# First batch's elementwise steps on VectorE, U and V converted in the first pair, later loads issued behind the turning transfers

## The chip, the cores and the metric

The kernel runs on one core of a Trainium2 chip. The metric is the device time of one execution in microseconds (us). The engines named below are TensorE (PE, with its weight loads as PEld), VectorE (DVE), ScalarE (ACT), GpSimd (POOL) and SyncE (SP, which here only issues transfers).

## What is computed

Three stages follow one another on four batches of 768 positions and 384 features. The first is a recurrence over time with a complex decay for each head and feature (its state is 48 x 48 for each of 8 heads), the second a mixing step of rank 32 (U and V) with a two-layer network, the third a two-dimensional Fourier transform, a normalisation and a second two-layer network:

```python
for t in range(S):                       # attention, q, k, v, a_re, a_im: (4, 8, 768, 48)
    S_re, S_im = ar*S_re - ai*S_im + kv, ar*S_im + ai*S_re     # a scaled to at most 0.999
    y[:, :, t] = einsum('bhd,bhde->bhe', q[:, :, t], S_re)
x = y.transpose(0, 2, 1, 3).reshape(B, S, H * D)
u = x + (x.transpose(0, 2, 1) @ U @ V).transpose(0, 2, 1)      # moe
x = u + relu(u @ w_ch1) @ w_ch2                                # w_ch1: 384 x 1536
u = x + real(fft(fft(x, axis=1), axis=2))                      # moe2
un = (u - mean(u)) / sqrt(var(u) + 1e-6)
out = u + relu(un @ w_ch1) @ w_ch2
```

## The kernel before

**Tiling.** Time is cut into 6 chunks of 128 positions for each batch, taken two at a time as a pair `m` (m = 0, 1, 2 are batch 0, m = 3, 4, 5 batch 1, and so on). For a pair, `decays(m)` makes the running products of the decay's size (a square, Ln, Exp, a scan along time, Ln, Exp) on tiles of 128 x 768 and multiplies q and k by them; `turns(m)` makes the running angle (Arctan, a scan, a reduction to one turn, Sin and Cos), and multiplies q and k by sine and cosine into one tile `QK` for each chunk. Six transfers for each chunk (`moved`, on SP's queue, the turning transfers) lay `QK` out again as `QT`. `products(m, j)` works on a chunk with TensorE: `scores` (tile `sc`), the mask (`pm`, VectorE), `kp` (a transpose of k, copied by ScalarE to a tile `k`), the output `y` from `pm` and from the state `S`, and the state's next value through `g`. The state runs from chunk to chunk: `S` of chunk c needs `S` of chunk c-1, and `y` of chunk c+1 needs `S` of chunk c and `QT` of chunk c+1.

**Order of the work.** Batch 0's attention is a preamble (`first_attention`): only when all its six chunks are done does the first network pass start. From then on the network's matmuls of batch b (`moe_units`: `hp`, `hh`, `hl`, `acc`) have the attention of batch b+1 woven between them. The instructions of each engine are put in order before the run by a scheduler that simulates the program with priorities; `tc.issue_after(i)` keeps one instruction behind another one, and `kept`, `tabled` and `behind` are helpers that use it. Each engine takes its instructions strictly in that order, so one that waits holds up all behind it. SP's queue too is one order for all loads, turning transfers and stores.

**Buffers that set the pace.** The weights `w` and also U and V come as pairs of 32-bit words, three tiles `st` in turn hold them (`stw0_f_z`: network 0, slice f of 12, half z), and `from_f64` turns them to floats: one step on ScalarE (`wx`), three on VectorE, then `load_w` splits them with ScalarE and GpSimd. The tiles `k` of the attention use the same three buffers. `QT` of chunk 5 lies in the buffer of chunk 2, that of chunk 4 in the buffer of chunk 1, so their transfers wait until `y` of chunk 2 and of chunk 1 is done. In batches after the first, the inputs `ain` and `qkin` have one buffer each.

**What the change touches.** `decays` has, for m = 2, a way of its own with squares on GpSimd, and `parts` of batch 0 that run on GpSimd (L402, L423, L424). `load_uv` is called inside `chunks()`, after the first pair. Loads (`fetch`, `load`, `load_v`) are plain `nc.sync.dma_start`, placed on SP by the scheduler. 20 and 36 `warm` matmuls stand at set places in TensorE's order.

Of the kernel before, what the change touches and what calls it, by code (L numbers as in the profile page):

```python
# [23 lines left out]
NC = 6  # L24
# [22 lines left out]
def mixer_kernel(ctx, tc, a_in, qk_in, v_in, u_in, v4_in, w_in, cc_in, ss_in, cb_in, sb_in, id_in, mask_in, rows_in, out):  # L47
# [75 lines left out]

    def fetch(src, name):
# [145 lines left out]
    def load(kind, m):  # L270
# [9 lines left out]
        nc.sync.dma_start(t, {"a": a_in, "qk": qk_in}[kind][b, cs[0] // 2])  # L280
# [26 lines left out]
    def parts(m):  # L307

        return [slice(0, 1), slice(1, 2)] if m == 0 else [slice(0, 2)]

    def decays(m):
# [26 lines left out]
        at_once = b or m in (0,1,)  # L338

        def sooner(m, *args, **kw):  # L340

            if m == 3:
                with tc.issue_after(last[0]):
# [11 lines left out]
        def least_re(js):  # L355

            (re,) = of(js, a[:, 0])
            V.tensor_scalar(unread(js), re, RE_LEAST, 0.0, ALU.is_ge, ALU.add, accum_out=stat("re", b, cc[js.start]))

        def most_im(js):  # L360
            (s2_,) = of(js, s2)
            V.tensor_scalar(unread(js), s2_, IM_MOST**2, 0.0, ALU.subtract, ALU.max, accum_out=stat("im", b, cc[js.start]))

        for js in jj:
            re, im, s1_, s2_ = of(js, a[:, 0], a[:, 1], s1, s2)
            if at_once:
                if b == 0:
                    V.scalar_tensor_tensor(out=s2_, in0=im, scalar=0.25, in1=im, op0=ALU.mult, op1=ALU.mult)
                else:
                    sooner(m, s2_, im, AF.Square, scale=0.5)  # L370
                sooner(m, s1_, re, AF.Square, accum_out=stat("big", b, cc[js.start]))
                if m == 0:
                    steady(js)
                else:
                    unused = unread(js) if b == 0 else Th[:, :, js]
                    sooner(m, unused, re, AF.Relu, bias=least, scale=-1.0, accum_out=stat("im", b, cc[0]))
                    sooner(m, unused, s2_, AF.Relu, bias=most, accum_out=stat("im", b, cc[1]))
                V.scalar_tensor_tensor(out=s1_, in0=s2_, scalar=4.0, in1=s1_, op0=ALU.mult, op1=ALU.add)
            else:
                (V if m == 0 else G).tensor_tensor(s2_, im, im, ALU.mult)  # L380
# [903 lines left out]
```

## Time and profile before

| | us |
|---|---|
| median of 3 runs (lowest, highest) | 955.83 (954.43, 956.68) |
| the profiled execution | 958.05 |
| its span, first to last instruction | 956.2 |
| PE busy | 827.8 (87%) |
| DVE, ACT, POOL busy | 605.2, 409.0, 238.1 |

The profile's 40 slices of 23.9 us show TensorE at 0 to 2 tenths busy in the first three slices, at 7 to 8 up to about 220 us and at 8 or 9 from there. The first network matmul (`hp`) stands at 150.08 us. The chain of work that ended last is by line mostly network matmuls (six lines of 6% each); the preamble has its place in the rest of it. A row of a timeline gives the start, the duration, the engine, the line, the operation, output and inputs with shapes, and in brackets the idle time of the engine before it with what ended it.

### The profile page before, as it was taken

The numbers are of one execution on the slowest core, as the hardware profiler recorded it, in microseconds if no ns is written. First come the engines' busy times: TensorE is split into PE (matmuls) and PEld (weight loads), VectorE is DVE, ScalarE is ACT, GpSimd is POOL, SyncE is SP. The second block draws the span as 40 slices with busy tenths as digits, with TensorE's granted clock in tenths as the row PEclk, the third lists the DMA queues.
The fourth block names the chain that finished last, engine by engine and source line by source line (L and its number), as shares of the span: only waits on it lengthen the run. The fifth ranks groups of instructions, "written<-read, shape, count | busy, mean of one in ns | idle before, by whom it ended". The sixth has DMA issues, their size and how long they took to land.

```text
span 956.2 us, 16800 instructions
## 1 busy us (share of the span) xinstructions
PE 827.8 (87%) x6686; PEld 564.4 (59%) x6686; DVE 605.2 (63%) x1118; ACT 409.0 (43%) x769; POOL 238.1 (25%) x289
## 2 busy tenths in 40 slices
PE   0227678778898899999999999899999999999997
PEld 0216565546575676566775566567666765766664
DVE  5795869786568677667347757853556666574121
ACT  5556347765567875674232443322112212211111
POOL 2060335542012121201027334711321322110000
PEclk9997689988899998999999999999999999999999
DMA  9508454836727765573336331300210111000000
GB/s 367 69 5 114 130 142 144 172 74 107 142 66 119 141 110 136 83 106 85 68 119 221 109 100 60 99 25 1 67 55 13 50 35 50 1 26 26 2 25 28
DMA packets 47095, 83.43 MB, mean 87 GB/s; under 512 B 5600, under 2 KB 36064, under 8 KB 47008
## 3 DMA queue, kind: packets, MB, share of 16 engines
q1 hardware_dynamic: 45152, 75.96, 34.5%
q0 software_dynamic: 1856, 6.31, 1.8%
q8 instruction: 54, 0.88, 0.4%
q14 instruction: 33, 0.27, 0.1%
HBM read 53.79 MB, written 9.44 MB: 66 GB/s over the span
## 4 chain that ended last, share of the span: by engine, by line
PE 48%; DVE 18%; ACT 8%; DMA 7%; issue 4%; POOL 3%; SPq 2%; DVEq 0%; POOLq 0%; ACTq 0%
PE acc L212 6%; PE acc L213 6%; PE hp L103 6%; PE hp L104 6%; PE hp L105 6%; PE acc L198 6%; DMA stw<-in_w_dram 3%; PE sc L530 3%; DMA QT<-QK 2%; ACT ls L99 2%; SPq L445 2%; DVE ls L404 2%; PE y L555 2%; DVE hl L231 1%; ACT turn L99 1%
## 5 line engine op out<-in xcount | busy, mean ns | idle before, releaser
L231 DVE SCALAR_TENSOR_TENSOR hl<-hp,hh 128x384 f16<-128x384 f32 x192 | 105.2, 551 | 177.3 <-ACT hh L230 176.7
L230 ACT ACTIVATE hh<-hp 128x384 f16<-128x384 f32 x192 | 93.0, 487 | 273.9 <-PE hp L105 250.9
L212 PE MATMUL acc<-w,hh 128*128 128x384 f16 x576 | 191.0, 332 | 5.3 <-ACT hh L230 5.3
L213 PE MATMUL acc<-w,hh 128*128 128x384 f16 x576 | 190.5, 331 | 1.7 <-POOL w L166 1.7
L198 PE MATMUL acc<-w,hl 128*128 128x384 f16 x576 | 128.0, 330 | 0.0
L103 PE MATMUL hp<-u,w 128*128 128x384 f16 x288 | 94.7, 330 | 10.9 <-DVE hl L231 8.0
L103 PE MATMUL hp<-n,w 128*128 128x384 f16 x288 | 94.0, 326 | 2.3 <-DVE hl L231 2.3
L530 PE MATMUL sc<-QT 96*128 96x128 f32 x384 | 66.2, 329 | 34.1 <-DMA QT<-QK 19.2
L104 PE MATMUL hp<-u,w 128*128 128x384 f16 x288 | 95.4, 331 | 0.0
L105 PE MATMUL hp<-u,w 128*128 128x384 f16 x288 | 95.2, 331 | 0.0
L105 PE MATMUL hp<-n,w 128*128 128x384 f16 x288 | 94.0, 326 | 0.0
L104 PE MATMUL hp<-n,w 128*128 128x384 f16 x288 | 93.9, 326 | 0.0
L104 PEld LDWEIGHTS <-w 128*128 128x128 f16 x576 | 56.7, 98 | 48.3 <-issue 13.7
L212 PEld LDWEIGHTS <-hh 128*128 128x128 f16 x576 | 56.8, 99 | 46.1 <-ACT hh L230 9.2
L530 PEld LDWEIGHTS sc<-QT 96*128 96x128 f32 x384 | 59.1, 234 | 40.1 <-issue 27.2
L198 PEld LDWEIGHTS <-hl 128*128 128x128 f16 x576 | 56.8, 99 | 39.0 <-issue 1.9
L103 PEld LDWEIGHTS <-w 128*128 128x128 f16 x576 | 56.5, 98 | 39.4 <-issue 3.1
L105 PEld LDWEIGHTS <-w 128*128 128x128 f16 x576 | 56.6, 98 | 37.5 <-issue 1.0
L213 PEld LDWEIGHTS <-hh 128*128 128x128 f16 x576 | 57.0, 99 | 32.7 <-issue 2.1
L540 PE MATMUL kp<-ident,QK 128*128 128x128 f32 x120 | 23.2, 317 | 51.3 <-DVE QK L497 35.9
L164 ACT ACTIVATE w<-wxw 128x384 f16<-128x384 f32 x48 | 24.8, 522 | 63.9 <-DVE wxw L143 63.8
L165 POOL TENSOR_SCALAR wxw<-wxw 128x384 f32<-128x384 f32 x48 | 33.1, 690 | 73.1 <-ACT w L164 72.5
(276 smaller groups left out, 1569.3 us busy)
## 6 DMA issues: line engine op xcount, KB each, us to landing
QT<-QK SPq DMA_DIRECT2D x144, 129.0 KB
stw<-in_w_dram SPq DMA_DIRECT2D x48, 384.0 KB
ain<-in_a_dram SPq DMA_DIRECT2D x12, 768.0 KB
qkin<-in_qk_dram SPq DMA_DIRECT2D x12, 768.0 KB
x1d<-x SPq DMA_DIRECT2D x24, 192.0 KB
vin<-in_v_dram SPq DMA_DIRECT2D x18, 192.0 KB
lo<-x1d SPq DMA_DIRECT2D x12, 192.0 KB
out_dram<-lo SPq DMA_DIRECT2D x12, 192.0 KB
```

Source lines behind the costliest of these rows:

```text
L99: ordered(lambda: A.activation(*args, **kw))
L103: T.matmul(o, ah, bh, start=start, stop=False, skip_group_check=skip)
L104: T.matmul(o, ah, bl, start=False, stop=False, skip_group_check=skip)
L105: T.matmul(o, al, bh, start=False, stop=stop, skip_group_check=skip)
L164: A.activation(w[:, 0, zs], x, AF.Copy, scale=WP[z])
L165: G.tensor_scalar(x, x, WP[z], 0.0, ALU.mult, ALU.add)
L198: T.matmul(acc[t], hl[:, t * 128 : (t + 1) * 128], w2h, start=False, stop=f == FB - 1 and extra is None)
L212: T.matmul(acc[t], hh[:, ts], w2h, start=f == 0, stop=False)
L213: T.matmul(acc[t], hh[:, ts], w2l, start=False, stop=False)
L230: A.activation(hh, hp, AF.Relu)
L231: V.scalar_tensor_tensor(out=hl, in0=hp, scalar=0.0, in1=whole_of(hh), op0=ALU.max, op1=ALU.subtract)
L530: T.matmul(ps[:, h, :], q[:, 128:256], q[:, :128], start=True, stop=True)
```

## The change

1. Batch 0's elementwise steps leave GpSimd: the squares and the sum of m = 2 take the same way as those of m = 1, and L402, L423 and L424 of batch 0 run on VectorE. Batches 1 to 3 keep GpSimd there.
2. In the first pair the check `steady` goes behind the sum on VectorE; the square at L412 of batch 0 is put into ScalarE's fixed order, ahead of the angles' table load; the checks with Relu of m = 1, 2 come behind it.
3. U and V are loaded right behind the first pair's inputs, ahead of those of pairs 1 and 2, and converted while the first pair is worked on.
4. Every load written down after the first turning transfer (`later`) is issued behind the last turning transfer that the program has written down by then.
5. `turns(2)` is woven one step behind `turns(1)`, and `decays(3)` starts 8 steps later in the program.

```diff
+    def later(to, x):
+        if lastqt[0] in nc.cur_bb.bb.instructions:
+            with tc.issue_after(lastqt[0]):
+                nc.sync.dma_start(to, x)
+        else:
+            nc.sync.dma_start(to, x)
...
-        nc.sync.dma_start(st.rearrange("p n w -> p (n w)"), src.bitcast(I32))
+        later(st.rearrange("p n w -> p (n w)"), src.bitcast(I32))
...
-        nc.sync.dma_start(t, {"a": a_in, "qk": qk_in}[kind][b, cs[0] // 2])
+        later(t, {"a": a_in, "qk": qk_in}[kind][b, cs[0] // 2])
...
-            nc.sync.dma_start(t, v_in[b, c])
+            later(t, v_in[b, c])
...
-            if m == 3:
-                with tc.issue_after(last[0]):
+            if m == 3 or m in (1, 2) and args[2] == AF.Relu:
+                with tc.issue_after(last[0] if m == 3 else squared[0]):
...
+            V.scalar_tensor_tensor(out=s1_, in0=s2_, scalar=4.0, in1=s1_, op0=ALU.mult, op1=ALU.add)
+            if m == 0:
+                with tc.issue_after([i for i in nc.cur_bb.bb.instructions if i.engine == V.engine][-1]):
                     steady(js)
...
-            else:
-                (V if m == 0 else G).tensor_tensor(s2_, im, im, ALU.mult)
-                A.activation(s1_, re, AF.Square, accum_out=stat("big", b, cc[js.start]))
-                (G if m == 2 else V).tensor_tensor(s1_, s1_, s2_, ALU.add)
-                most_im(js)
...
-            (V if m == 0 else G).tensor_tensor(t, im, th, ALU.mult)
+            (G if b else V).tensor_tensor(t, im, th, ALU.mult)
...
-            A.activation(th, s2_, AF.Square, scale=2.0)
+            if b == 0:
+                tabled(th, s2_, AF.Square, scale=2.0)
+                if m == 0:
+                    squared[0] = last[0]
+            else:
+                A.activation(th, s2_, AF.Square, scale=2.0)
...
-            (G if m in (1, 2) else V).tensor_tensor(f, q, s1_, ALU.mult)
-            (V if m == 0 else G).tensor_tensor(g, k, s2_, ALU.mult)
+            V.tensor_tensor(f, q, s1_, ALU.mult)
+            (G if b else V).tensor_tensor(g, k, s2_, ALU.mult)
...
     def first_attention(w1):
+        with tc.high_priority(-800):
+            load_uv()
         run(decays(0), turns(0))
...
-            anchor()
-            with tc.high_priority(-800):
-                load_uv()
...
-            yield from chain(turns(1), turns(2))
+            yield from zipped(turns(1), late(1, turns(2)))
             anchor()
-            yield from decays(3)
+            yield from late(8, decays(3))
...
-    for m in range(3):
+    load("a", 0)
+    load("qk", 0)
+    early_words = [fetch(u_in, "u")] + [fetch(v4_in[:, z * 384 : (z + 1) * 384], f"v{z}") for z in range(2)]
+    for m in (1, 2):
```

The order shows what becomes of this on each engine. First ScalarE at the program's start, where `ls0_0` is the first pair's running tile, `ain0_0`, `ain0_2` and `ain0_4` the inputs of pairs 0, 1 and 2, and `wxu`, `wxv` the words of U and V. Before:

```order
L346 ACTIVATE ls0_0_134,stats_80<-ain0_0_112 128x768
L99 ACTIVATE ls0_0_134<-ls0_0_134 128x768 x2
L99 ACTIVATE ain0_0_112<-ain0_0_112 128x768
L346 ACTIVATE ls0_2_204,stats_80<-ain0_2_116 128x768
L346 ACTIVATE un1_209,stats_80<-ain0_2_116,least_86 128x768
L390 ACTIVATE ls0_0_134<-ls0_0_134 128x768
```

And after:

```order
L356 ACTIVATE ls0_0_161,stats_80<-ain0_0_112 128x768
L122 ACTIVATE wxu_140<-stu_116 128x192
L122 ACTIVATE wxv0_147<-stv0_118 128x384
L616 CAST ust_88<-wxu_140 128x6x96
L122 ACTIVATE wxv1_154<-stv1_120 128x384
L621 CAST vst_89<-wxv0_147 128x384
L356 ACTIVATE ls0_2_231,stats_80<-ain0_2_122 128x768
L99 ACTIVATE ls0_0_161<-ls0_0_161 128x768
L621 CAST vst_89<-wxv1_154 128x384
L99 ACTIVATE ls0_0_161<-ls0_0_161 128x768
L99 ACTIVATE ain0_0_112<-ain0_0_112 128x768
L386 ACTIVATE ls0_0_161<-ls0_0_161 128x768
```

The first Ln of pair 0 (the first L99 row) now stands behind U, most of V and the square of pair 1's input.

Next SP's queue, from the turning transfers of chunk 3 on (`QT0_3` is batch 0, chunk 3; `stw0_1_0` is slice 1, half 0 of network 0's weights). Before:

```order
L445 DMA QT0_3_353<-QK0_3_352 16x8x258 x6
L127 DMA stw0_0_0_551<-in_w_dram 128x768
L445 DMA QT0_4_419<-QK0_4_418 16x8x258 x6
L127 DMA stw0_0_1_553<-in_w_dram 128x768
L280 DMA ain1_2_464<-in_a_dram 128x1536
L280 DMA qkin1_2_496<-in_qk_dram 128x1536
L127 DMA stw0_1_0_564<-in_w_dram 128x768
L127 DMA stw0_1_1_658<-in_w_dram 128x768
L445 DMA QT0_5_431<-QK0_5_430 16x8x258 x6
L127 DMA stw0_2_0_669<-in_w_dram 128x768
```

And after:

```order
L443 DMA QT0_3_360<-QK0_3_359 16x8x258 x6
L443 DMA QT0_4_371<-QK0_4_370 16x8x258 x6
L443 DMA QT0_5_389<-QK0_5_388 16x8x258 x6
L129 DMA ain1_2_517<-in_a_dram 128x1536
L129 DMA qkin1_2_575<-in_qk_dram 128x1536
L129 DMA stw0_0_0_543<-in_w_dram 128x768
L129 DMA stw0_0_1_545<-in_w_dram 128x768
L129 DMA stw0_1_0_556<-in_w_dram 128x768
L129 DMA vin1_0_798<-in_v_dram 128x384
L129 DMA stw0_1_1_657<-in_w_dram 128x768
L129 DMA stw0_2_0_668<-in_w_dram 128x768
```

Four weight tiles and the two inputs of pair 4 have moved from ahead of chunk 5's transfers to behind them, and so has `vin1_0`, a load of the kernel's first 15 us.

Last VectorE in the preamble's middle, where `S0_1` is the state after chunk 1 and the steps on `ls1_0` and `turn1_0` are `decays(3)`. Before:

```order
L404 SCALAR_TENSOR_TENSOR ls1_0_442<-starts_103,ls1_0_442 128x768
L436 TENSOR_TENSOR pm0_2_456<-sc0_2_0_457,mask_82 128x512
L413 SCALAR_TENSOR_TENSOR turn1_0_441<-ls1_0_442,turn1_0_441 128x768
L436 TENSOR_TENSOR pm0_2_456<-sc0_2_1_466,mask_82 128x512
L417 SCALAR_TENSOR_TENSOR ls1_0_442<-turn1_0_441,ls1_0_442 128x768
L378 SCALAR_TENSOR_TENSOR ls1_2_1266<-ls1_2_1266 128x768
L418 SCALAR_TENSOR_TENSOR ls1_0_442<-ls1_0_442 128x768
L419 COPY fe1_0_444<-ls1_0_442 128x6
L423 TENSOR_TENSOR ls1_0_442<-qkin1_0_132,ls1_0_442 128x768
L436 SCALAR_TENSOR_TENSOR S0_1_574<-g0_1_531,S0_0_416 96x384
L120 TENSOR_SCALAR stw0_0_0_551<-stw0_0_0_551 128x384
L608 TENSOR_TENSOR S0_1_574<-S0_1_574,fe0_1_368 96x384
```

And after:

```order
L412 SCALAR_TENSOR_TENSOR turn1_0_460<-ls1_0_461,turn1_0_460 128x768
L434 SCALAR_TENSOR_TENSOR S0_1_566<-g0_1_519,S0_0_437 96x384
L416 SCALAR_TENSOR_TENSOR ls1_0_461<-turn1_0_460,ls1_0_461 128x768
L606 TENSOR_TENSOR S0_1_566<-S0_1_566,fe0_1_386 96x384
L417 SCALAR_TENSOR_TENSOR ls1_0_461<-ls1_0_461 128x768
L418 COPY fe1_0_463<-ls1_0_461 128x6
L422 TENSOR_TENSOR ls1_0_461<-qkin1_0_138,ls1_0_461 128x768
L434 SCALAR_TENSOR_TENSOR S0_2_678<-g0_2_637,S0_1_566 96x384
L606 TENSOR_TENSOR S0_2_678<-S0_2_678,fe0_2_478 96x384
L434 TENSOR_TENSOR pm0_0_275<-sc0_4_0_682,mask_82 128x512
L434 TENSOR_TENSOR pm0_0_275<-sc0_4_1_687,mask_82 128x512
L376 SCALAR_TENSOR_TENSOR ls1_2_1265<-ls1_2_1265 128x768
```

`S0_1` has come forward by four rows of `decays(3)` and one of pair 4, and pair 4's sum (`ls1_2`, L376) has gone from ahead of it to behind both states, where the weights' conversions follow it.

## Rows read from the trace of the kernel before

**Rows 1.** Stretches: length; busy us (count) PE, PEld, DVE, ACT, POOL; clock; DMA; GB/s

```profile
200.00:300.00 100.00, 86.56 (x860) 60.78 (x859) 65.52 (x97) 65.04 (x111) 18.76 (x20) 0.93 0.61 113
...
500.00:956.00 456.00, 440.64 (x2826) 283.43 (x2825) 261.61 (x615) 113.56 (x244) 116.06 (x152) 1.00 0.17 54
```

**Rows 2.** Timeline of VectorE, pair 0

```profile
8.86 0.96 DVE L368 SCALAR_TENSOR_TENSOR ls<-ain 128x768 f32<-128x768 f32 x1 [0.84 <-DMA ain<-in_a_dram]
...
13.02 1.93 DVE L391 SCALAR_TENSOR_TENSOR ls<-ls 128x768 f32<-128x768 f32 x1 [0.69 <-ACT ls L390]
...
15.74 3.35 DVE L404 TENSOR_TENSOR_SCAN ls<-starts,ls 128x768 f32<-128x768 uint8 x1
...
24.10 0.96 DVE L413 SCALAR_TENSOR_TENSOR ain<-ls,ain 128x768 f32<-128x768 f32 x1 [3.28 <-ACT ain L412]
```

**Rows 3.** Timeline of GpSimd, the first square of pair 2

```profile
12.67 1.47 POOL L380 TENSOR_TENSOR ls<-ain 128x768 f32<-128x768 f32 x1 [9.91 <-DMA ain<-in_a_dram]
```

**Rows 4.** Timeline of ScalarE, pair 0

```profile
8.06 1.72 ACT L99 ACTIVATE ls<-ls 128x768 f32<-128x768 f32 x2 [1.94 <-DVE ls L378]
...
23.24 0.83 ACT L412 ACTIVATE ain<-ls 128x768 f32<-128x768 f32 x1
```

**Rows 5.** Timeline of VectorE, 42 to 74 us

```profile
41.93 1.76 DVE L404 TENSOR_TENSOR_SCAN ls<-starts,ls 128x768 f32<-128x768 uint8 x1
44.81 2.20 DVE L391 SCALAR_TENSOR_TENSOR ls<-ls 128x768 f32<-128x768 f32 x1 [1.12 <-ACT ls L390]
...
51.44 2.61 DVE L417 SCALAR_TENSOR_TENSOR ls<-ain,ls 128x768 f32<-128x768 f32 x1
...
56.77 3.32 DVE L464 TENSOR_TENSOR_SCAN ain<-going,ain 128x768 f32<-128x768 uint8 x1
...
66.11 1.01 DVE L143 SCALAR_TENSOR_TENSOR wxv<-stv,wxv 128x384 int32<-128x384 int32 x2
...
72.04 0.96 DVE L497 TENSOR_TENSOR QK<-qkin,ain 128x768 f32<-128x768 f32 x1
```

**Rows 6.** Timeline of SP's queue

```profile
89.15 4.57 SPq L445 DMA_DIRECT2D QT<-QK  x6
...
115.82 3.81 SPq L445 DMA_DIRECT2D QT<-QK  x6
120.16 41.56 SPq L127 DMA_DIRECT2D stw<-in_w_dram  x15
```

**Rows 7.** Timeline of TensorE: scores of chunk 2, y from the state, first network matmul

```profile
82.85 3.76 PE L530 MATMUL sc<-QT 96*128 96x128 f32 x16 [5.82 <-DMA QT<-QK]
...
87.11 1.90 PE L555 MATMUL y<-S,QT 96*64 96x48 f32 x30
...
111.77 1.91 PE L555 MATMUL y<-S,QT 96*64 96x48 f32 x32
...
150.08 0.33 PE L103 MATMUL hp<-u,w 128*128 128x384 f16 x1
```

**Rows 8.** Timeline of VectorE: a step of pair 3, state after chunk 1, weight tile 2_0

```profile
102.65 0.96 DVE L413 SCALAR_TENSOR_TENSOR turn<-ls,turn 128x768 f32<-128x768 f32 x1 [2.93 <-ACT turn L412]
...
109.43 0.54 DVE L436 SCALAR_TENSOR_TENSOR S<-g,S 96x384 f32<-96x384 f32 x1
...
125.68 0.36 DVE L120 TENSOR_SCALAR stw<-stw 128x384 int32<-128x384 int32 x1 [3.08 <-DMA stw<-in_w_dram]
```

**Rows 9.** Chain of work that ended last: start us, us, what

```profile
73.97 0.55 SPq L445
...
81.83 7.94 DMA stw<-in_w_dram
...
132.49 4.61 DMA stw<-in_w_dram
...
185.70 3.06 DMA stw<-in_w_dram
```

**Rows 10.** Timeline of ScalarE behind the turning transfers of batch 1

```profile
180.95 0.56 ACT L120 ACTIVATE wxw<-stw 128x384 f32<-128x384 f32 x1 [5.64 <-DMA stw<-in_w_dram]
```

More of the change, by code (lines that the diff above doesn't have):

```diff
@@ L122, in kept @@
             fn(*args, **kw)
+    lastqt = [None]
+    def later(to, x):
[4 more added lines that the diff above has]
+            nc.sync.dma_start(to, x)
     def fetch(src, name):
@@ L309, in parts @@
         return [slice(0, 1), slice(1, 2)] if m == 0 else [slice(0, 2)]
+    squared = [None]
     def decays(m):
@@ L353, in steady @@
             )
[L355 to L362, printed above, removed]
         for js in jj:
             re, im, s1_, s2_ = of(js, a[:, 0], a[:, 1], s1, s2)
-            if at_once:
-                if b == 0:
-                    V.scalar_tensor_tensor(out=s2_, in0=im, scalar=0.25, in1=im, op0=ALU.mult, op1=ALU.mult)
-                else:
-                    sooner(m, s2_, im, AF.Square, scale=0.5)
-                sooner(m, s1_, re, AF.Square, accum_out=stat("big", b, cc[js.start]))
-                if m == 0:
-                    steady(js)
[L374 to L379, printed above, removed]
-                (V if m == 0 else G).tensor_tensor(s2_, im, im, ALU.mult)
-                A.activation(s1_, re, AF.Square, accum_out=stat("big", b, cc[js.start]))
-                (G if m == 2 else V).tensor_tensor(s1_, s1_, s2_, ALU.add)
-                most_im(js)
@@ new lines, in decays @@
+            if b == 0:
+                V.scalar_tensor_tensor(out=s2_, in0=im, scalar=0.25, in1=im, op0=ALU.mult, op1=ALU.mult)
+            else:
+                sooner(m, s2_, im, AF.Square, scale=0.5)
+            sooner(m, s1_, re, AF.Square, accum_out=stat("big", b, cc[js.start]))
+            if m:
+                unused = unread(js) if b == 0 else Th[:, :, js]
+                sooner(m, unused, re, AF.Relu, bias=least, scale=-1.0, accum_out=stat("im", b, cc[0]))
+                sooner(m, unused, s2_, AF.Relu, bias=most, accum_out=stat("im", b, cc[1]))
@@ L391, in decays @@
             V.scalar_tensor_tensor(out=s1_, in0=s1_, scalar=0.999**2, in1=s2_, op0=ALU.min, op1=ALU.mult)
-            if not at_once:
-                least_re(js)
         yield
@@ L411, in decays @@
             tabled(s2_, s2_, AF.Exp, bias=lnhalf, scale=-0.5, accum_out=stat("decay", b, cc[js.start]))
-            A.activation(th, s2_, AF.Square, scale=2.0)
+            if b == 0:
+                tabled(th, s2_, AF.Square, scale=2.0)
+                if m == 0:
+                    squared[0] = last[0]
+            else:
+                A.activation(th, s2_, AF.Square, scale=2.0)
             V.scalar_tensor_tensor(out=th, in0=s1_, scalar=FSCALE**2, in1=th, op0=ALU.mult, op1=ALU.mult)
@@ L621, in load_uv @@
             zs = slice(z * 384, (z + 1) * 384)
-            vr = from_f64(v4_in[:, zs], f"v{z}")
+            vr = from_f64(v4_in[:, zs], f"v{z}", early_words[1 + z])
             A.copy(vst[:, zs], vr)
```

4 lines of the change are left out of this document (1 added, 3 removed).

## The prediction

> **What bounds the kernel now.** I read the stretches first. From 200 us on TensorE is busy 87 of 100 us, and from 500 us 441 of 456 [rows 1]: the change leaves the instructions there as they are, so time can be won only ahead of it. The first network matmul stands at 150.08 us [rows 7]; whatever comes before it delays everything behind it one for one, and what I forecast is by how much it comes forward. Then I read the timelines of the preamble for who waits last, and find three links. One is VectorE from 42 to 72 us, where products on GpSimd stretch its own steps: a scan takes 1.76 us alone and 3.32 beside them [rows 5]. The second is the state after chunk 1, which VectorE makes at 109.43 us behind all of pair 3's decay steps [rows 8]; y of chunk 2 waits for it (111.77, [rows 7]), and so do chunk 5's turning transfers, whose buffer y frees (115.82, [rows 6]). The third is the weights: behind those transfers 15 tiles go out in a row [rows 6], and tile 2_0 keeps VectorE idle for 3.08 us until 125.68 [rows 8], with the last states of the chain in the rows behind it.
>
> **Pair 0.** U and V (983 KB, 1.25 times an input of 786 KB) now go ahead of pair 1's input. Two inputs take 3.81 us (8.86 to 12.67, [rows 2, 3]), so U and V take 2.4, and pair 1's input lands at 11.3, not 8.86. ScalarE's order puts its square ahead of pair 0's first Ln, which starts at 12.2 and not at 8.06 [rows 4]: 4.1 late. From there to L391 three checks and a square (2.5 us) are no longer between, a cast is, so L391 comes at 16.0 for 13.02: +3.0. Then VectorE has GpSimd off its back: L391 0.96 for 1.93 and the scan 1.76 for 3.35 [rows 2] (the first of the GpSimd rows beside them is that of [rows 3]), -2.6; one more step, L368 of pair 2, +0.9; and the square L412 goes ahead of the table load and two arctans, -2.2. Sum -0.9: L413 at 23.2 for 24.10. Bounds: +1.0 if the input lands another 1.9 late, -3.3 if U and V cost no load time. The conversions (nine steps on VectorE and three) lie in waits of that stretch; if that cover fails they cost up to 2 us, which the upper bound takes in. The checks moved behind the square run while VectorE turns angles, and nobody waits for them.
>
> **Pairs 1 and 2, to chunk 2's QK (72.04, [rows 5]).** Gone from VectorE: the stretch of five steps, 1.2 + 1.65 + 1.6 + 1.55 + 1.6 = 7.6 us (L391 2.20, L417 2.61 and L464 3.32 are shown, the small copies L483 and L463 took 1.78 and 1.77; alone they take 0.96, 0.96, 1.76, 0.16 and 0.16), and the conversions of U and V, 4.6 us (of four kinds of step, three take 1.0 for V's two tiles, as L143 shows, and one 0.6; U's are a third of that). Added: six products of 0.95, 5.7. Some of it lies beside waits for ScalarE, whose order and length there hardly change. Laid out step by step, with ScalarE's rows as they are, QK comes at 64.9: -7.2. The ends: -5 if half of the stretch was hidden under ScalarE's waits, -8.
>
> **Pair 3 and the state after chunk 1.** Chunk 2's transfers take 8.9 us from issue to scores (73.97 to 82.85, [rows 9, 7]), so scores at 75.7. y of chunk 1 from the state ended at 89.0 [rows 7], 6.2 behind the scores' start; now a transpose and two more pieces stand between, 8.9, so 84.6. Pair 3's chain on ScalarE has a copy that waits for that y, and no longer has one that waits for weight tile 0_0 [rows 9]: its step L413 (102.65, [rows 8]) comes at 95.5. The state now stands right behind it, no longer behind six rows with a product of 2.45 beside GpSimd: 96.4 for 109.43. g and y of chunk 2 follow as before, 4.1 later, and chunk 5's transfers go out at 100.5, not 115.82: -15.3, of which 2.1 is that SP no longer holds them behind two weight tiles.
>
> **What is late next.** The weights and pair 4's inputs stand behind those transfers now, and this is the new wait: VectorE's order has pair 4's sum, then tile 0_0, ahead of the mask of chunk 3. From the issue of chunk 5's transfers I count: landed +8.9; pair 4's two inputs 1.9 each, three weight tiles 0.95 each, +15.5; their conversion with two masks on VectorE, tile 1_0 done at +19; its buffer takes 2_0, which lands alone in 3.06 [rows 9], with its neighbour in 3.5: +22.5, so 123.0 for 125.68 [rows 8]. Of 15 us 2.7 are left. Behind it the order is as before; scores and z of chunks 3 and 5, which held TensorE until 129, are done earlier, which gives up to 2.4 more. I take 1.3, and 4.0 in all: the first network matmul at 146.
>
> That transfers queue behind one another I read from a row: tile 0_0, issued at 81.83 behind chunk 3's transfers, took 7.94 us where one alone takes 3.06 [rows 9]. The Trainium skill (DMA: Bandwidth & Descriptors, section "Two DMAs through the same engine are not ordered") says that descriptors of one queue start in order but are pipelined, and that nothing orders transfers across the 16 engines; by that the inputs need not wait for the turning transfers, and the time would be that of the second rival. The trace here agrees with waiting.
>
> **The first network pass.** Tile 9_0 has moved from ahead of chunks 0 and 1 of batch 1 (12 turning transfers) to behind them. Three tiles, no longer two, land behind those. ScalarE sat 5.64 us until 180.95 for the first of them [rows 10]; the third will land about 1 us later than the second did, and its conversions add 1.4 us on VectorE, where slices 9 and 10 wait for them. I take +1.0; ends 0 (TensorE has other waits there) and +3. `vin` loads, now behind the turning transfers, land long before their y and cost nothing; without that slack, 0.5 us each.
>
> **Sum.** -4.0 + 1.0 = -3.0 on the profiled execution's 958.05, 955.05; against the median of 955.83, which lies 2.2 below it, 952.8.
>
> **Rivals.** *The buffers' rhythm eats it:* a tile takes 4.61 us to land where the queue is busy (132.49, [rows 9]), not 3.06. Two rounds of the three buffers lie between tile 0_0 and the last state, so 3.1 back, which leaves +0.1: 955.9. For it: the three buffers turn without pause from 120 us on. Against it: the slow landing had other tiles in front. Chance 0.25.
>
> *The loads overtake:* pair 4's inputs and the first tiles land without waiting for chunk 5's transfers. Tile 2_0 then comes up to 4 us earlier: 948.8. [Rows 9] speaks against it. Chance 0.08.
>
> *The weights become the bound, and the kernel is slower:* all depends on when chunk 5's transfers go out, since tile 2_0 lands 22.5 behind that. The 1.3 from TensorE less the 1.0 of tile 9_0 lets 2_0 land as late as 126.0 without loss, so an issue after 103.5 makes the kernel slower. With pair 0 at its upper bound (+1.9 against my sum) and half of pair 1's gain lost (+2.2) they go out at 104.6; tile 2_0 lands at 127.1, +1.4, and without help from TensorE and with the upper end of the network pass (+3) the time is 955.83 + 4.4 = 960.2. For it: pair 0's Ln is held by a load in the order itself. Chance 0.15.
>
> **How the numbers follow.** Forecast 0.52 (950 to 953.9), overtaking 0.08, rhythm 0.25, slower 0.15. About 0.2%, 1.9 us, is what a measurement of this kernel can tell from no change. Faster: 0.52 + 0.08 = 0.60; same 0.25; slower 0.15. The range leaves out the far parts of the second and the last: 948.5 to 958.
>
> **What would show it.** In the profile after: pair 0's first Ln near 12 and L412 near 23 us on VectorE; no stretched steps and QK of chunk 2 near 65; the state after chunk 1 near 96; chunk 5's transfers out near 100; VectorE idle for pair 4's input around 106 to 112; tile 2_0 at 123; the first `hp` near 146. If `hp` is early and the end is not, slices 9 to 11 have taken it back. If QK is not early, the stretch was hidden, and the second step is wrong. A first Ln at 8 would mean that the loads don't bind.

## The result, and the profile after

The changed kernel is slower: a median of 961.62 us (960.21 to 963.62, 11 runs) against 955.83, a ratio of 1.0062 with a 95% interval of 1.0046 to 1.0078. The forecast was 952.8, with a range of 948.5 to 958.0. The profiled execution after has a span of 960.3 us, the one before 956.2. A second measurement on another chip (e16, below) gave 1.0052 (1.0037 to 1.0068).

Timeline of ScalarE after (columns as ahead of the prediction), as in [rows 4]: the first Ln of pair 0, and the wait for pair 4's input.

```profile
12.25 0.83 ACT L99 ACTIVATE ls<-ls 128x768 f32<-128x768 f32 x1
...
110.98 1.57 ACT L356 ACTIVATE ls<-ain 128x768 f32<-128x768 f32 x2 [9.29 <-DMA ain<-in_a_dram]
```

Timeline of VectorE after, as in [rows 2, 5, 8]:

```profile
23.05 0.96 DVE L412 SCALAR_TENSOR_TENSOR ain<-ls,ain 128x768 f32<-128x768 f32 x1 [2.12 <-ACT ain L99]
...
45.51 1.75 DVE L398 TENSOR_TENSOR_SCAN ls<-starts,ls 128x768 f32<-128x768 uint8 x1
...
64.12 0.96 DVE L495 TENSOR_TENSOR QK<-qkin,ain 128x768 f32<-128x768 f32 x1 [3.14 <-ACT ain L99]
...
96.25 0.55 DVE L434 SCALAR_TENSOR_TENSOR S<-g,S 96x384 f32<-96x384 f32 x1
...
112.68 0.96 DVE L376 SCALAR_TENSOR_TENSOR ls<-ls 128x768 f32<-128x768 f32 x1 [4.00 <-ACT ls L356]
...
123.80 0.36 DVE L120 TENSOR_SCALAR stw<-stw 128x384 int32<-128x384 int32 x1 [3.56 <-DMA stw<-in_w_dram]
...
133.73 0.54 DVE L434 SCALAR_TENSOR_TENSOR S<-g,S 96x384 f32<-96x384 f32 x1
```

The last of these rows is the state after chunk 4; before:

```profile
134.31 0.54 DVE L436 SCALAR_TENSOR_TENSOR S<-g,S 96x384 f32<-96x384 f32 x1
```

SP's queue after, as in [rows 6]. The first row joins all transfers of chunks 2 to 5; the last six, chunk 5's, went out from 100.59 on, behind y of chunk 2, which ended at 100.50.

```profile
66.05 38.33 SPq L443 DMA_DIRECT2D QT<-QK  x24
104.48 0.53 SPq L129 DMA_DIRECT2D ain<-in_a_dram  x1
...
105.56 1.37 SPq L129 DMA_DIRECT2D stw<-in_w_dram  x3
107.24 0.33 SPq L129 DMA_DIRECT2D vin<-in_v_dram  x1
119.84 39.61 SPq L129 DMA_DIRECT2D stw<-in_w_dram  x15
```

TensorE after, as in [rows 7]: scores and y of chunk 2, the warming matmuls, the first network matmul.

```profile
74.89 3.76 PE L528 MATMUL sc<-QT 96*128 96x128 f32 x16 [8.90 <-DMA QT<-QK]
...
98.59 1.91 PE L553 MATMUL y<-S,QT 96*64 96x48 f32 x32
...
140.33 6.34 PE L1024 MATMUL warm<-ident,mask 128*128 128x256 f16 x36
...
149.22 0.33 PE L103 MATMUL hp<-u,w 128*128 128x384 f16 x1
```

Up to chunk 5's transfers the preamble went as forecast, some 15 us ahead of before. Then the rows show the waits that took it back: VectorE 4.00 us for pair 4's sum, then 3.56 us for a weight tile. At the first network matmul 0.86 us are left, and at the second network's first matmul (625.4 before, 629.2 after) the kernel is 3.8 us behind, 4.7 us lost on the way. So two things have to be found: where 14 us of the preamble went, and where the 4.7 behind it went.

One thing can be read from the program without a run. The prediction speaks of the order in the preamble and around tile 9_0 alone. Over the whole program, some 480 of TensorE's 5446 instructions and some 145 of VectorE's would have to be moved to turn the one order into the other, the last of them in the pass of batch 3 (the network pass that goes over batch 3): the network and the attention of all later batches are woven in another way.

### The profile page after: what moved, and what is told of

The parts are those of the page before. It is cut to its first block, busy times and chain, and to the rows that moved or that the text cites. A ratio compares the mean times of both kernels' runs of the same rounds, so it can differ in the third digit from the quotient of the medians.

```text
span 960.3 us, 16811 instructions
## 1 busy us (share of the span) xinstructions
PE 825.0 (86%) x6686; PEld 562.1 (59%) x6686; DVE 598.1 (62%) x1122; ACT 411.0 (43%) x773; POOL 225.6 (23%) x281
## 4 chain that ended last, share of the span: by engine, by line
PE 49%; DVE 22%; DMA 11%; ACT 9%; issue 4%; SPq 2%; POOL 2%; DVEq 0%; ACTq 0%; POOLq 0%
PE acc L221 6%; PE acc L207 6%; PE hp L103 6%; PE acc L222 6%; PE hp L105 6%; PE hp L104 6%; DMA QT<-QK 4%; DMA ain<-in_a_dram 3%; DMA stw<-in_w_dram 3%; PE sc L528 2%; ACT ls L99 2%; SPq L443 2%; DVE wxw L151 2%; DVE ls L398 2%; DVE hl L240 1%
## 5 line engine op out<-in xcount | busy, mean ns | idle before, releaser
L528 PE MATMUL sc<-QT 96*128 96x128 f32 x384 | 63.3, 316 | 32.6 <-DMA QT<-QK 19.3
L528 PEld LDWEIGHTS sc<-QT 96*128 96x128 f32 x384 | 56.7, 223 | 38.2 <-issue 24.6
L581 POOL TENSOR_SCALAR fe<-QT 96x8 f32<-96x8 f32 x20 | 12.5, 627 | 197.9 <-DMA QT<-QK 136.7
```

The costliest lines, as they stand in the source:

```text
L528: T.matmul(ps[:, h, :], q[:, 128:256], q[:, :128], start=True, stop=True)
```

## The experiments

All ratios are to the kernel before, measured beside it on the same chip; 0.001 is 1 us. The kernel with plain loads (e2) is the base of most: the changed kernel with `later` doing nothing. Its network passes have the order of the kernel before on every engine.

**Which loads: e1, e2, e3.** `pre[0]` is true until `first_attention` has been written down.

```diff
-        if lastqt[0] in nc.cur_bb.bb.instructions:
+        if pre[0] and lastqt[0] in nc.cur_bb.bb.instructions:        # e1
+        if False:                                                    # e2
+        if not pre[0] and lastqt[0] in nc.cur_bb.bb.instructions:    # e3
```

> The changed kernel, with the loads issued behind the turning transfers in the preamble alone; from the first network pass on they are plain again, and the order of the network passes is that of the kernel before on every engine. Theory A, the re-woven network passes cost what was lost: the preamble stays as in the changed kernel (first network matmul within 1 us of 149.2), and the rest takes as long as in the kernel before, so 955.8 - 0.9 = about 955, 0.993 of the changed kernel. Theory B, the loss comes with what the preamble leaves behind (inputs and weights of batch 1 that are later, buffers in another rhythm): the time stays near 961.

> The changed kernel with no load held back at all: four weight tiles and the first input of pair 4 stand as before among the turning transfers of chunks 2 to 5, and the network passes have the order of the kernel before. Theory A (network order costs 5, the held loads cost the preamble its gain): chunk 5's transfers go out between 100 and 105 us, weight tile 2_0 no longer waits behind them, the first network matmul comes at 142 to 147, and the time is 949 to 953. Theory B (the weights' own chain of three buffers sets the preamble's end, wherever they are issued): the first network matmul stays at 149 to 150 and the time is that of the first of these runs, about 955.

> The changed kernel with the loads held back in the network passes alone; in the preamble they are plain, as in the second of these runs, and the network passes have the order of the changed kernel. Theory A (the order of the network passes costs about 5): the time is that of the second of these runs plus 4 to 6, so 953 to 959. Theory B (the held loads of the preamble cost): the time is that of the second of these runs within 1 us.

Measured: e1 0.9976 (0.9963 to 0.9990), e2 0.9904 (0.9885 to 0.9922), e3 0.9946 (0.9926 to 0.9966). By the times theory A holds in all three: holding the loads costs 7 us in the preamble and 4 in the network, and without it the rest of the change is worth 9 us. (The first network matmul of e1 stands at 146.46 and not within 1 us of 149.2; the last group of experiments takes that up.) In e2 the first tiles and pair 4's input go out among the turning transfers, and chunk 5's transfers lose nothing by it. SP's queue and TensorE of e2:

```profile
62.37 0.34 SPq L131 DMA_DIRECT2D stw<-in_w_dram  x1
66.10 21.45 SPq L443 DMA_DIRECT2D QT<-QK  x18
87.66 0.52 SPq L131 DMA_DIRECT2D stw<-in_w_dram  x1
91.05 0.33 SPq L131 DMA_DIRECT2D ain<-in_a_dram  x1
99.09 0.33 SPq L131 DMA_DIRECT2D stw<-in_w_dram  x1
100.77 3.80 SPq L443 DMA_DIRECT2D QT<-QK  x6
```

```profile
133.49 5.97 PE L1024 MATMUL warm<-ident,mask 128*128 128x256 f16 x36
...
142.03 0.33 PE L103 MATMUL hp<-u,w 128*128 128x384 f16 x1
```

The first network matmul comes at 142.03, 8 us ahead of before and 7.2 ahead of the changed kernel, though chunk 5's transfers go out at the same time in both.

**Preamble, inputs or weights: e8, e9.** `w` is true for weight tiles.

```diff
+        if pre[0] and not w and lastqt[0] in nc.cur_bb.bb.instructions:    # e8: inputs, v
+        if pre[0] and w and lastqt[0] in nc.cur_bb.bb.instructions:        # e9: weights
```

> The changed kernel with the weights plain everywhere and plain loads in the network passes, but pair 4's inputs and the first v of batch 1 held behind chunk 5's turning transfers in the preamble. Theory A, it is the weights behind chunk 5's transfers that cost the preamble its gain: the first network matmul comes at 141 to 143 us as with plain loads, and the time is 948 to 951. Theory B, it is VectorE's wait for pair 4's first input: the first network matmul comes at 146 to 149.5, the time is 953 to 956.

> The other half: in the preamble the weights alone are held behind chunk 5's turning transfers; pair 4's input stands ahead of them as with plain loads. Its network passes have the order of the changed kernel in nearly all places. Theory A (weights): the first network matmul at 146 to 149.5; with 5 for the order of the network passes 957 to 961. Theory B (pair 4's input): the first network matmul at 141 to 143, 952 to 955.

Measured: e8 0.9912 (0.9892 to 0.9932), e9 0.9989 (0.9975 to 1.0004). TensorE of e8, then of e9:

```profile
136.99 0.33 PE L103 MATMUL hp<-u,w 128*128 128x384 f16 x1
```

```profile
147.95 0.32 PE L103 MATMUL hp<-u,w 128*128 128x384 f16 x1 [0.65 <-ACT u L673]
```

It is the weights. With pair 4's inputs behind and the weights ahead the network even starts 5 us earlier than in e2. (To be compared here are the first matmuls: the time of e9 also has the new order of the network passes in it.) VectorE still waits for pair 4's input, as the row of e8 shows, but with three weight tiles converted and the states after chunks 1 and 2 made ahead of it, and that costs nothing. The 5 us are not in the time: see the first pass, below.

```profile
113.22 0.96 DVE L377 SCALAR_TENSOR_TENSOR ls<-ls 128x768 f32<-128x768 f32 x1 [3.31 <-ACT ls L357]
```

**Network, tile 9_0 or inputs and v: e4, e5.**

```diff
+        if not pre[0] and w and lastqt[0] in nc.cur_bb.bb.instructions:        # e4: weights
+        if not pre[0] and not w and lastqt[0] in nc.cur_bb.bb.instructions:    # e5: inputs, v
```

> The changed kernel with plain loads, but the weights that are written down from the first network pass on (tile 9_0 and those behind it) held behind the turning transfers of batch 1; inputs and v stay plain, and the order of the network passes is otherwise nearly that of the kernel before. Theory A, tile 9_0 behind 12 turning transfers is what costs the 4 us of the held loads in the network (slices 9 to 11 wait): time of the plain loads, 949.2, plus 3 to 5, so 952 to 954. Theory B, the re-weaving of attention and network through all passes costs it: 949 to 950.5.

> The changed kernel with plain loads, but the inputs and v of the network passes held behind the turning transfers; tile 9_0 stays ahead of them, and the network passes have the order of the changed kernel in all but a few places. Theory A of the run before (tile 9_0): 949 to 950.5. Theory B (re-weaving): 952 to 954.

Measured: e4 0.9920 (0.9890 to 0.9950), e5 0.9946 (0.9927 to 0.9965). Tile 9_0 costs 1.5 us by the ratios (0.9920 for 0.9904), which their intervals don't tell from nothing; inputs and v cost the whole 4. The program narrows it: held inputs alone change no engine's order, held v alone gives that of e5, row for row.

**Late data or another order: e12, e13.** `vb` is the batch of a load of v, and 0 for other loads.

```diff
+        if not pre[0] and vb==1 and lastqt[0] in nc.cur_bb.bb.instructions:    # e12
+        if not pre[0] and vb>=2 and lastqt[0] in nc.cur_bb.bb.instructions:    # e13
```

> The changed kernel with plain loads, but the v of batch 1 held behind the turning transfers; those of batches 2 and 3 are plain. On TensorE 393 instructions of the three passes of batches 0 to 2 stand elsewhere than with plain loads, as in the run with all v held. Theory A, the order costs it: the stretch from the first network matmul of batch 2 to the second network takes about 203 us, where the plain order takes 200 to 201.5, though no load of batch 2 or 3 is held there; the ratio to the kernel before is 0.993 to 0.996 (0.9904 with plain loads, 0.9946 with all v held). Theory B, v that lands later costs it: 200 to 201.5 us in that stretch and a ratio of 0.990 to 0.992.

> The changed kernel with plain loads, but the v of batches 2 and 3 held behind the turning transfers; only the queue that issues them has another order, every other engine's is that of the plain loads. Theory A (order): the stretch from batch 2 on 200 to 201.5 us, the ratio 0.9885 to 0.992 as with plain loads. Theory B (late v): about 203 us there and a ratio of 0.993 to 0.996.

Measured: e12 0.9936 (0.9923 to 0.9949), e13 0.9930 (0.9912 to 0.9948). By the times e12 goes with the order. e13, taken by its two numbers, goes with late data: 0.9930, and 202.9 us from batch 2 on. What its 202.9 us are made of says otherwise. The pass of batch 2 (from its first `hp` to that of batch 3) has its end woven with the last attention; its last quarter (from the 163rd of its 216 `hp` on), by the view of stretches (columns as in [rows 1]), in before, after, e12 and e13:

```profile
515.42:538.03 22.61, 19.84 (x127) 12.45 (x125) 19.51 (x40) 7.77 (x16) 12.93 (x16) 1.00 0.24 71
```

```profile
516.83:541.68 24.85, 20.69 (x130) 13.10 (x129) 21.91 (x42) 8.46 (x17) 11.79 (x16) 1.00 0.21 64
```

```profile
506.57:531.44 24.87, 20.69 (x131) 13.10 (x129) 21.88 (x42) 8.45 (x17) 11.80 (x16) 1.00 0.22 64
```

```profile
504.92:530.26 25.34, 22.83 (x125) 13.79 (x124) 21.89 (x46) 7.96 (x16) 13.31 (x16) 0.87 0.23 63
```

After and e12 are alike to 0.1 us in every column of times, at full clock, though e12's v is plain in that pass: it is the order, and TensorE stands idle 4.2 us there (24.85 - 20.69) for 2.8 before. e13 is as long, but for another reason: a granted clock of 0.87, with 2.5 us idle as before. The whole pass of batch 2 in all of these, from the same view ("low clock" is busy time times one less the granted clock):

| pass of batch 2, us | before | e18 | e2 | e13 | after | e16 | e3 | e5 | e12 | e9 |
|---|---|---|---|---|---|---|---|---|---|---|
| order | old | old | old | old | new | new | new | new | new | new |
| length | 112.7 | 115.5 | 112.7 | 115.4 | 115.7 | 116.1 | 116.0 | 115.5 | 115.7 | 115.4 |
| idle TensorE | 4.6 | 4.3 | 4.6 | 4.3 | 7.1 | 7.5 | 7.3 | 7.7 | 7.0 | 7.5 |
| low clock | 1.7 | 4.7 | 1.7 | 4.7 | 1.9 | 1.9 | 1.9 | 0.0 | 1.9 | 0.0 |
| VectorE's step `f` from `ye`, 91 us into the pass | 0.36 | 0.36 | 0.36 | 0.36 | 3.27 | 3.29 | 3.28 | 3.27 | 3.27 | 3.28 |

Idle time parts the two orders, whichever loads are held there: 7.0 to 7.7 us with the new one, 4.3 to 4.6 with the old (3.8 to 5.7 in the other runs that have it). So about 3 us are the order, shown in a pass where e12 and e9 hold no load; e9 holds none in any network pass, and from batch 1 on its TensorE order is that of the changed kernel in every place. In its profile e13 lost 3 us to the clock, as the kernel before did in e18, where no load is held at all. Over its six runs e13 has a mean granted clock of 0.958, for 0.9625 in those of e2. That its 2.5 us by the ratios (1.0 by the medians) are the clock alone is not shown; it stays open.

The passes of batches 0 and 1 have to be taken together, since the new order also moves some of VectorE's work from the second into the first: alone they take 147 to 151 and 126 to 129 us with the new order, 139 to 145 and 132 to 135 with the old one in these runs, together 273.7 to 278.4 and 274.2 to 277.6. There no cost of the order shows beyond what two profiles of one program differ by.

Where the idle stands, in TensorE's timeline at the end of the pass of batch 2, after and then before: slices wait for VectorE's `hl`, which has the first steps of the transform and the second network's weights at the same place.

```profile
522.04 0.32 PE L103 MATMUL hp<-u,w 128*128 128x384 f16 x1 [1.54 <-DVE hl L240]
...
526.42 0.32 PE L103 MATMUL hp<-u,w 128*128 128x384 f16 x1 [1.19 <-DVE hl L240]
...
530.49 0.32 PE L103 MATMUL hp<-u,w 128*128 128x384 f16 x1 [0.57 <-DVE hl L240]
...
533.37 0.34 PE L221 MATMUL acc<-w,hh 128*128 128x384 f16 x1 [0.88 <-ACT hh L239]
```

```profile
526.47 0.32 PE L103 MATMUL hp<-u,w 128*128 128x384 f16 x1 [1.42 <-DVE hl L231]
...
529.45 0.36 PE L103 MATMUL ac<-cc,eeh 128*128 128x194 f32 x1 [1.35 <-ACT eeh L890]
```

One step of VectorE ahead of the first of these waits differs in every run with the new order and in no other (last line of the table). VectorE and GpSimd after, then VectorE before:

```profile
516.95 3.27 DVE L860 TENSOR_TENSOR f<-ye 128x192 f32<-128x192 f32 x1
```

```profile
519.01 0.99 POOL L875 TENSOR_TENSOR x<-x,x 128x384 f32<-128x384 f32 x1
```

```profile
516.88 0.36 DVE L863 TENSOR_TENSOR f<-ye 128x192 f32<-128x192 f32 x1 [0.42 <-POOL ye L876]
```

In the new order this step starts while GpSimd is in a row of steps without a pause that ends at 520.00, and its own row ends at 520.22. It is the kind of stretch that the change takes out of the preamble (e6, below), set up anew in a network pass by the order alone. That these 2.9 us are all of the 3 was not tried, since no run takes that step alone out of GpSimd's way.

And no matmul waits for v. Of the changed kernel, the instructions from 180 to 500 us that read or load v, and what ended the idle time ahead of them (us, times; the longest): no row of that view is a DMA, nor is one in e5 and e12, and e3 has one of 0.7 us.

```profile
its engine sat idle before it (us, times) until:
  ACT k L545: 7.7, 7
  issue: 3.8, 13
```

**The parts of the preamble's gain: e6, e7, e10, e14.** Each undoes one part of e2; e14 does one part alone on the kernel before.

```diff
-            (G if b else V).tensor_tensor(t, im, th, ALU.mult)                  # e6 (e14 the other way round,
+            (V if m == 0 else G).tensor_tensor(t, im, th, ALU.mult)             #     with the squares of m = 2)
-            V.tensor_tensor(f, q, s1_, ALU.mult)
+            (G if m in (1, 2) else V).tensor_tensor(f, q, s1_, ALU.mult)
-            (G if b else V).tensor_tensor(g, k, s2_, ALU.mult)
+            (V if m == 0 else G).tensor_tensor(g, k, s2_, ALU.mult)
...
-            yield from zipped(turns(1), late(1, turns(2)))                      # e7
+            yield from chain(turns(1), turns(2))
-            yield from late(8, decays(3))
+            yield from decays(3)
...
-        with tc.high_priority(-800):                                            # e10: load_uv() back into chunks(),
-            load_uv()                                                           #      its loads behind the inputs
```

> The changed kernel with plain loads and six elementwise products of batch 0 (pairs 1 and 2) on GpSimd again, as in the kernel before. Theory A, the stretch beside GpSimd was what VectorE lost: products of queries and keys of chunk 2 come at 66 to 69 us instead of 64.2, everything behind them as much later, and the time is 951 to 954. Theory B, that stretch lay under waits: chunk 2 within 0.5 us of 64.2 and the time 949 to 950.

> The changed kernel with plain loads, with the angles of pair 2 behind those of pair 1 and pair 3's decay steps where they were. Theory A, pair 3's steps ahead of the state after chunk 1 hold it: the state comes at 99 to 105 us instead of 96.5 and the time is 951 to 956. Theory B, the state waits for the chain on ScalarE in any case: it stays within 1 us, and so does the time, 948.5 to 950.

> The changed kernel with plain loads, but U and V are loaded behind the inputs and converted among chunk 1's work, as in the kernel before. Theory A, converting them in the first pair's waits is a gain: pair 0 comes out about 1 us earlier or later than now, but queries and keys of chunk 2 come at 66 to 69 us for 64.2, and the time is 951 to 953. Theory B, what pair 0 loses to their loads is what chunk 2 saves: 948 to 950.5.

> The kernel before, with batch 0's squares and products on VectorE and nothing else of the change: loads, U and V, the order of ScalarE's squares and of the rows are the old ones. Theory A, this part carries the preamble's gain: products of queries and keys of chunk 2 come at 63 to 67 us for 72.0, the first network matmul at 133 to 144, and the ratio to the kernel before is 0.985 to 0.992. Theory B, the gain needs the other parts too (U and V early, pair 3 later): the first network matmul at 146 to 150 and a ratio of 0.995 to 1.

Measured: e6 0.9948 (0.9928 to 0.9967), chunk 2's product at 68.10 (64.17 in e2), the first network matmul at 144.1: theory A. e7 0.9914 (0.9895 to 0.9932), the state after chunk 1 at 100.9 instead of 96.5 and the first network matmul at 141.3: the state did come later, as A has it, and the time did not, as B has it, so neither theory was whole. e10 0.9882 (0.9861 to 0.9904), chunk 2's product at 63.6 and the first network matmul at 132.7: both theories fall, since the old place of U and V is no worse and perhaps 2 us better (the intervals overlap). e14 0.9910 (0.9896 to 0.9924), product at 65.9, first network matmul at 142.7: theory A, the move to VectorE alone brings what e2 has. Chunk 2's product in e6, then in e2:

```profile
68.10 0.96 DVE L495 TENSOR_TENSOR QK<-qkin,ain 128x768 f32<-128x768 f32 x1 [2.84 <-ACT ain L99]
```

```profile
64.17 0.96 DVE L495 TENSOR_TENSOR QK<-qkin,ain 128x768 f32<-128x768 f32 x1 [3.14 <-ACT ain L99]
```

How a step is stretched beside GpSimd is seen in e6, on VectorE and then GpSimd:

```profile
43.88 2.23 DVE L387 SCALAR_TENSOR_TENSOR ls<-ls 128x768 f32<-128x768 f32 x1 [1.06 <-ACT ls L386]
```

```profile
43.48 1.81 POOL L396 TENSOR_TENSOR ain<-ain 128x768 f32<-128x768 f32 x1
```

The step takes 0.96 us alone (at the same place in e2). GpSimd's product began first and ended at 45.29; 0.96 behind that is 46.25, and VectorE's row ends at 46.11. The Trainium skill (SBUF — State Buffer, section "SBUF: two separate sides") says that the port pair the two engines share is an exclusive lock, held for a whole instruction, when VectorE has two inputs in SBUF; this pair of rows agrees.

**An earlier start that brings less: e11, e15.** e11 cuts the warming matmuls ahead of the last transposes; e15 joins e8 and e10.

```diff
-    for after, n in zip(scored[:1] + ends, [20, 36, 0, 0, 0, 20]):
+    for after, n in zip(scored[:1] + ends, [20, 16, 0, 0, 0, 20]):    # e11
```

> The changed kernel with plain loads, and 16 for 36 of the warming matmuls ahead of the last transposes of the preamble; with it the order of attention and network changes in many places again. Theory A, the warming matmuls keep the first network matmul waiting (with plain loads the 36 end at 139.5, the operand they stand in front of is made at 135.4): the first network matmul comes at 138 to 139.5, and the time follows by 1 to 3 if the clock granted behind them stays at its upper level. Theory B, the clock is at the lower level behind them and takes it back: 948.5 to 951. In either case the length from the first network matmul to the second network's first one, 473.6 to 476.1 us with one order and 480.0 to 481.3 with the other so far, shows what a third order costs.

> The changed kernel with U and V loaded and converted as before, the weights and the later loads plain, and pair 4's inputs behind chunk 5's turning transfers: the two variants with the earliest first network matmul (132.7 and 137.0) in one. Theory A, the first network matmul still sets the end: it comes at 128 to 133 and the ratio falls to 0.984 to 0.988. Theory B, the first pass is now bound by its weight tiles, and an earlier start only waits for them: the ratio stays at 0.987 to 0.991, with the first pass 65 us or longer to its second half, for 59.8 in the kernel before.

Measured: e11 0.9932 (0.9912 to 0.9953), first network matmul at 139.6; e15 0.9892 (0.9872 to 0.9913), at 134.3. Neither beats its base, and e11's time lies outside both of its theories. From the first network matmul to the start of batch 0's second half takes 59.8 us before and 60.0 in e2, but 66.1 in e8 and e15, 64.7 in e10 and 70.5 in e11, with 14 to 18 us of TensorE idle for 10. So e15 falls to theory B as far as the length goes; what it waits for there is a mixture (`hl`, chunk 0's turning transfers, weights, the state of chunk 1). These programs have another order there too: in batch 0's pass some 80 instructions of TensorE stand elsewhere than in e2 in e8 and e15, 50 in e10 and 260 in e11. So whether an earlier start waits for its weights or is held by its order is not told apart. e11's third order costs 10 us in that half, wins 5 of them back in the next and is the quickest from batch 2 on (199.2 us to the second network, for 200 to 204), which no theory here foretold.

**What doesn't add up: e16, e17, e18.** The changed kernel, e1 and the kernel before once more, unchanged, on one chip.

> The changed kernel once more. Theory A, the lower clock at the 36 warming matmuls goes with the execution: they take anything from 4 to 6.4 us here, and the first network matmul comes at 146.5 to 149.5. Theory B, it goes with the program: 6.2 to 6.4 us and 149.2 within 0.3 again. The ratio to the kernel before is 1.004 to 1.008 in both cases.

> The first of these runs once more (loads held in the preamble alone). Theory A (the clock goes with the execution): the 36 warming matmuls take anything from 4 to 6.4 us, the first network matmul comes at 146.4 to 149.4. Theory B (with the program): 4.1 us and 146.5 within 0.3 again. The ratio to the kernel before is 0.996 to 0.999.

> The kernel before once more, for a second profile of it. Theory A (the clock goes with the execution): the 36 warming matmuls, 6.21 us in the profile before, take 4 to 6.3 us and the first network matmul comes 0 to 2.2 us ahead of 150.1. Theory B (with the program): 6.2 us and 150.1 within 0.3.

Measured: e16 1.0052 (1.0037 to 1.0068), e17 0.9979 (0.9957 to 1.0001). The 36 warming matmuls, in e16, e1, e17 and e18:

```profile
140.35 4.09 PE L1024 MATMUL warm<-ident,mask 128*128 128x256 f16 x36
```

```profile
139.69 4.09 PE L1026 MATMUL warm<-ident,mask 128*128 128x256 f16 x36
```

```profile
140.72 6.34 PE L1026 MATMUL warm<-ident,mask 128*128 128x256 f16 x36
```

```profile
140.49 4.09 PE L1024 MATMUL warm<-ident,mask 128*128 128x256 f16 x36
```

Theory A: it goes with the execution. The first network matmul stands at 147.2, 149.6 and 147.2 (e16, e17, e18) for 149.2, 146.5 and 150.1 of the same three programs earlier, in e17 and e18 by 0.2 and 0.7 us outside the ranges of theory A. Batch 0's second half starts at 210.8 and 210.6 in the two profiles of the changed kernel: what the one gains at the start it has lost by then.

The profile of e16 also has what the tiles 1_1, 2_0 and 2_1 took from their issue (120.19 to 121.87) to their landing:

```profile
DMA to landing us min/median/max: 4.2/4.3/4.5
```

The sum stays open: holding in the preamble costs 7 us, in the network 4, and both together 14 to 15. The 3 to 4 us too many are about what the intervals of the four ratios allow together (3.3 to 3.7 us, an estimate from them), so there may be nothing to explain. Against it, e9, which has held weights in the preamble and the new order as well, lies at 0.9989, some 3 us below such a sum and 6 to 7 below the changed kernel, though its network starts within 1.3 us of it. From e9 the changed kernel differs by the held inputs and v, and by some 110 places of TensorE in batch 0's pass. By the stretches the changed kernel and e1, with the same preamble, are 8 to 9 us apart at the end of batch 0's pass (batch 1 starts at 298.0 in both profiles of the one, at 289.0 and 290.4 in the other's), and the pass of batch 1 gives 4 to 7 of it back. Behind the plain preamble it is much the same (e3 and e2: 290.5 and 284.6, with 3.5 given back), so the profiles don't show where the rest comes from.

The quickest version is e10, 946.62 us against 958.46 on its chip, 0.9882 of the kernel before: the steps on VectorE, pair 3 later, plain loads, U and V where they were. Its interval (0.9861 to 0.9904) overlaps those of e2, e14 and e15.

## Why the prediction was wrong

- **Pair 0 to the state after chunk 1: right.** Ln at 12.25 (12.2 was forecast), L412 at 23.05 (23.2), QK of chunk 2 at 64.12 (64.9), its scores at 74.89 (75.7), the state at 96.25 (96.4), chunk 5's transfers from 100.5 on (100.5). e6 and e14 show that the second step of the working, GpSimd off VectorE's back, carries it. U and V early only move time about: they cost pair 0 some 4 us (L412 at 19.09 in e10) and win back a little less by chunk 2's product (63.58 in e10, 64.17 in e2). Two small slips in the working change nothing: the conversions' 4.6 us add up to 4.8 by the terms given, and chunk 5's transfers follow the state by 4.25 us (109.43 to 113.68 before), not 4.1.
- **The new wait: named rightly.** VectorE idle to 112.7 for pair 4's input, which landed at 111.0 (100.5 + 8.9 + 1.9 = 111.3 by the working), because a load issued behind turning transfers lands behind them. The Trainium skill's sentence (DMA: Bandwidth & Descriptors, "Two DMAs through the same engine are not ordered") that nothing orders transfers across the 16 DMA engines made a rival of 0.08; no run here shows such overtaking.
- **Tile 2_0 and what follows: the first failing step.** Forecast 123.0 for it and 146 for the first network matmul. The row at 123.80 is tile 1_1; it and 2_0 went out only from 119.84 on, when the conversions of 0_1 and 1_0 were ending, and 2_0's own conversion started at 124.86, 0.8 us ahead of before and not 2.7. The term that was too small is the landing of 2_0 beside its neighbours, 3.5 us: in e16, the changed kernel again, it and its two neighbours took 4.2 to 4.5 us (the row stands with e16 above), and 2_0 was there 24.3 us behind the issue of chunk 5's transfers, not 22.5. The 1.3 us from TensorE did not come at all: VectorE had two masks and the conversions of four tiles between there and the state after chunk 4 (133.73, for 134.31 before). That is the rival of the buffers' rhythm, which left 0.9 us at the first network matmul, as measured (in e16 and e18, the second profiles of both kernels, nothing is left), and which had the slow landing, 4.61 us, as its reason. The larger error was to price this against before and not against what the same preamble does with plain loads: 142.03.
- **"The change leaves the instructions there as they are": the second failing step, and the one that set the sign.** It was said of the network passes from their number, without comparing their order. The order was new for some 480 instructions of TensorE, and the term for the network, +1.0 for tile 9_0, has the right size for that tile (e4: 1.5, not told from nothing) and leaves out 4 us or more, 3 of them in the pass of batch 2 by idle time. The load that was said to cost nothing, `vin`, kept no matmul waiting in the changed kernel, and holding it was what turned the order over (e12). Without that (e1) the kernel would have come out at 0.9976, close to what was forecast.
- **"Whatever comes before the first network matmul delays everything behind it one for one": too simple.** It held to 0.2 us for e2 (8.0 earlier, and batch 0's second half 7.9 earlier), but e8 starts 5 us ahead of e2 and is 1.1 us behind it at that point, and e10 keeps 4.6 of its 9.3 over e2, both with another order there.
- **The slower rival** had nearly the time (960.2 for 961.62) and not the mechanism: it wanted chunk 5's transfers out after 103.5, and they went out at 100.59. That its number came close is luck.

## What to carry to other kernels

A step that costs nothing on the chip can still cost a few us through the planner that orders the program: after a change, compare the whole order of the busiest engine, not only the place that was edited, price a re-woven pass as an unknown of several us of either sign, and look in it for steps that now stand beside another engine's. To keep a transfer off a queue is a change of the order behind it as well; test the load's hold apart from the rest of the change, as it was here the whole loss. And before a chain is moved forward, look for the next resource at the same place: three buffers for weights that went out late gave back 14 of 15 us.

## Of the hardware, not expected

The same 36 matmuls in the same order took 4.09 us in one execution and 6.34 in another of the same program. Two stretches of 10 us (columns as in [rows 1]), the matmuls being in the second, in the changed kernel and in e16, which is the same program:

```profile
130.00:140.00 10.00, 5.65 (x83) 4.10 (x80) 8.01 (x12) 4.66 (x12) 5.06 (x7) 0.90 0.47 144
140.00:150.00 10.00, 10.00 (x65) 7.55 (x64) 8.12 (x16) 6.86 (x14) 5.18 (x7) 0.75 0.56 172
```

```profile
130.00:140.00 10.00, 7.09 (x106) 5.77 (x103) 7.98 (x12) 4.18 (x11) 4.97 (x8) 0.83 0.45 125
140.00:150.00 10.00, 9.47 (x75) 7.26 (x74) 9.53 (x16) 7.49 (x17) 5.52 (x7) 1.00 0.63 189
```

A granted clock of 0.75 means that half of that stretch ran at 1.2 GHz, and 1.00 that all of it ran at 2.4. TensorE was busy for 5.65 us of the 10 ahead of the one and for 7.09 ahead of the other. In e13 and e18 another 3 us went the same way in the pass of batch 2 (the table above), in programs whose order there is that of the kernel before. A difference of 3 us between two single profiles is therefore not yet a difference between two kernels; idle time by stretch was the steadier sign.
